# Start of a SwiGLU kernel: the four x chunks in three loads instead of four, used in another order

## The chip, the cores and the metric

The kernel runs on one core of a Trainium2 chip. The metric is the device time of one execution in microseconds, and the kernel is given the median over several runs. Besides the runs, one execution was recorded by the hardware profiler, and its views are what this document reads.

## The reference

The reference is a feed-forward layer with a gate. The inputs are bf16, and the sizes are 2048 rows of 640 values and a hidden width of 1536.

```python
B, S, D, F = 1, 2048, 640, 1536
g = silu(x @ w_gate)          # (S, F)
u = x @ w_up                  # (S, F)
return (g * u) @ w_down       # (S, D)
```

## The kernel before

All weights and the transposed x stay in the on-chip memory SBUF. The 2048 rows are worked on in four blocks (`sb`) of 512 rows, the hidden width in twelve columns of 128 (`fc`), and the contraction over 640 in five steps of 128 (`kd`). For each block and each `fc`, `proj` does five matmuls of 512 columns into the PSUM tile `pg` (gate) and five into `pu` (up), both on line 134. ScalarE computes `sg = silu(pg)` (line 180), and VectorE multiplies it by `pu` into `aT` (line 181). When a block's twelve columns are done, the down projection follows: the last 128 output columns first, transposed (`po_t`, line 189), and then 512 columns for each of four groups of rows (`po_a`, line 213). Then the next block begins.

The change lies in the first five microseconds, before that regular stream. The matmuls need x with the contraction dimension on the partitions. The blocks 1 to 3 get that by transposing loads (line 97). Block 0 would come too late that way, so its 512 rows are loaded plainly as four chunks of 128 rows (`load_x`, line 74, into `x_sb`). TensorE transposes each chunk in five 128x128 pieces (`transpose_chunk`, line 125) into a PSUM tile `pt`, and VectorE or ScalarE copies `pt` to `xT` (line 130). `pt` takes its space from the tags `po_a` and `po_b`, which have two buffers each. So the third tile of a tag waits until the copy of its first has freed the buffer.

Loads go out on two queues, SyncE's (`nc.sync`) and ScalarE's (`nc.scalar`). SyncE loads the chunks 0 and 1, and ScalarE the chunks 2 and 3. Behind them come the first 128 columns of `w_gate` and of `w_up`, each in two halves over the two queues (line 87). Then SyncE alone loads the further slices named by `W_CHUNKS` (line 71), gate and up by turns: columns 1 to 2 of `fc` (the second gate slice and the second up slice), then 3 to 5, 6 to 8 and 9 to 11. `w_down` and the transposed blocks of x follow. ScalarE also runs one small `Silu` (line 89), which makes it load its activation table early.

TensorE fills its waits with matmuls of ones into an unused tile (`warm`, line 103): `N_WARM` of them while x is on its way, `N_GAP` after the first two chunks, and two ahead of the first projection. The first gate projection goes over 256 columns at a time (`proj_pair`, line 149). Its first half takes the chunks 0 and 2 and its second half the chunks 1 and 3, since chunks 0 and 2 are the first loads of the two queues. `keep_order` holds TensorE's and ScalarE's instructions up to this point to the order in which they are written.

Of the kernel before, what the change touches and what calls it, by code (L numbers as in the profile page):

```python
# [10 lines left out]
def _body(  # L11
# [8 lines left out]
    nc = tc.nc  # L20
    P = nc.NUM_PARTITIONS
# [11 lines left out]
    KD = D // P  # L33
    KF = F // P
    S_BLK = 512
    NSB = S // S_BLK
    SUB = S_BLK // P
    DA = 512
    Q = 32
    N_WARM, N_GAP = 18, 4  # L40
    W_CHUNKS = [(0, 1), (1, 3), (3, 6), (6, 9), (9, 12)]
    assert D % P == 0 and F % P == 0 and S % S_BLK == 0 and D > DA and SUB == 4

# [9 lines left out]
    xT = consts.tile([P, KD, S], bf16)  # L53
    wg_sb = consts.tile([P, KD, F], bf16)
# [18 lines left out]
    def load_x(eng, c0, c1):  # L73
        eng.dma_start(out=x_sb[:, c0:c1, :], in_=x_v[:, c0:c1, :])
# [4 lines left out]

    queues = (nc.sync, nc.scalar)  # L80
    halves = ((0, KD // 2 + 1), (KD // 2 + 1, KD))
    for c in (0, 1):
        for i, eng in enumerate(queues):
            load_x(eng, c + 2 * i, c + 2 * i + 1)
    for dst, src in ((wg_sb, wg_v), (wu_sb, wu_v)):
        for eng, (k0, k1) in zip(queues, halves):
            eng.dma_start(out=dst[:, k0:k1, wslice(0, 1)], in_=src[:, k0:k1, wslice(0, 1)])
# [13 lines left out]
    def warm(n):  # L101
        for _ in range(n):
            nc.tensor.matmul(  # L103
                pw[:, 0:P], lhsT=ones[:], rhs=ones[:], start=True, stop=True
            )

    def keep_order(engine):

        traced = [i for i in nc.cur_bb.bb.instructions if i.engine == engine]
        for a, b in zip(traced, traced[1:]):  # L110
            tc.add_manual_dep(
                b,
                a.name,
                mybir.DependencyInfo(
                    mybir.DependencyClass.NoSync, mybir.DependencyReason.DATA
                ),
                reason="keep_order",
            )

    def transpose_chunk(c, parts):  # L120
        c_sl = slice(c * P, (c + 1) * P)
        for copy, tag, k0, k1 in parts:
            pt = psum.tile([P, k1 - k0, P], bf16, tag=tag, name="pt")
            for kd in range(k0, k1):
                nc.tensor.transpose(  # L125
                    out=pt[:, kd - k0, :],
                    in_=x_sb[:, c, kd * P : (kd + 1) * P],
                    identity=ident[:],
                )
            copy(out=xT[:, k0:k1, c_sl], in_=pt[:])  # L130

    def proj(ps, w_sb, fc, sb, c0, c1):
        for kd in range(KD):
            nc.tensor.matmul(  # L134
                ps[:, c0:c1],
                lhsT=w_sb[:, kd, fc * P : (fc + 1) * P],
                rhs=xT[:, kd, sb * S_BLK + c0 : sb * S_BLK + c1],
                start=(kd == 0),
                stop=(kd == KD - 1),
            )  # L140

    def proj_pair(ps, w_sb, fc, sb, b):


        def pair(ap):
            return ap.rearrange("p (a b c) -> p b a c", b=2, c=P)[:, b]

        for kd in range(KD):
            nc.tensor.matmul(  # L149
                pair(ps[:]),  # L150
                lhsT=w_sb[:, kd, fc * P : (fc + 1) * P],
                rhs=pair(xT[:, kd, sb * S_BLK : (sb + 1) * S_BLK]),
                start=(kd == 0),
                stop=(kd == KD - 1),
            )

    for sb in range(NSB):
        s_sl = slice(sb * S_BLK, (sb + 1) * S_BLK)
        for fc in range(KF):
            pg = psum.tile([P, S_BLK], f32, tag="gu", name="pg", bufs=4)  # L160
            pu = psum.tile([P, S_BLK], f32, tag="gu", name="pu", bufs=4)
            if sb == 0 and fc == 0:
                dve, act = nc.vector.tensor_copy, nc.scalar.copy
                warm(N_WARM)
                transpose_chunk(0, [(dve, "po_a", 0, KD)])
                transpose_chunk(2, [(dve, "po_b", 0, KD)])
                warm(N_GAP)
                for c in (1, 3):
                    transpose_chunk(c, [(act, "po_a", 0, 2), (dve, "po_b", 2, KD)])
                warm(2)  # L170
                proj_pair(pg, wg_sb, fc, sb, 0)
                proj_pair(pg, wg_sb, fc, sb, 1)
                proj(pu, wu_sb, fc, sb, 0, S_BLK)
                keep_order(mybir.EngineType.PE)
                keep_order(mybir.EngineType.Activation)
            else:
                proj(pg, wg_sb, fc, sb, 0, S_BLK)
                proj(pu, wu_sb, fc, sb, 0, S_BLK)
            sg = work.tile([P, S_BLK], f32)
            nc.scalar.activation(sg[:], pg[:], ACT.Silu)  # L180
            nc.vector.tensor_tensor(  # L181
                out=aT[:, fc, s_sl], in0=sg[:], in1=pu[:], op=ALU.mult
            )


        n_t = (SUB if sb < NSB - 1 else SUB - 1) * P
        po_t = psum.tile([P, n_t], f32, tag="po_b", name="po_t")
        for kf in range(KF):
            nc.tensor.matmul(  # L189
                po_t[:],  # L190
                lhsT=wd_sb[:, kf, DA:D],
                rhs=aT[:, kf, sb * S_BLK : sb * S_BLK + n_t],
                start=(kf == 0),
                stop=(kf == KF - 1),
            )
        ot_t = outp.tile([P, n_t], bf16, name="ot_t")
        ot_q = outp.tile([P, n_t], bf16, name="ot_q")
        nc.scalar.copy(ot_t[:], po_t[:])  # L198
        nc.vector.transpose(out=ot_q[:], in_=ot_t[:])  # L199
        for q in range(P // Q):  # L200
            nc.scalar.dma_start(
                out=out2[
                    sb * S_BLK : sb * S_BLK + n_t, DA + q * Q : DA + (q + 1) * Q
                ].rearrange("(i r) c -> r i c", r=Q),
                in_=ot_q[q * Q : (q + 1) * Q, :].rearrange("r (i c) -> r i c", c=Q),
            )

        for j in range(SUB):
            s0 = sb * S_BLK + j * P
            last = sb == NSB - 1 and j == SUB - 1  # L210
            po_a = psum.tile([P, DA], f32, tag="po_a", name="po_a")
            for kf in range(KF):
                nc.tensor.matmul(  # L213
                    po_a[:],
                    lhsT=aT[:, kf, s0 : s0 + P],
                    rhs=wd_sb[:, kf, 0:DA],
                    start=(kf == 0),
                    stop=(kf == KF - 1),
                )
            ot = outp.tile([P, DA], bf16, name="ot")  # L220
            nc.scalar.copy(ot[:], po_a[:])  # L221
            nc.sync.dma_start(out=out2[s0 : s0 + P, 0:DA], in_=ot[:])
            if last:
                po_b = psum.tile([P, D - DA], f32, tag="po_b", name="po_b")
                for kf in range(KF):
                    nc.tensor.matmul(  # L226
                        po_b[:],
                        lhsT=aT[:, kf, s0 : s0 + P],
                        rhs=wd_sb[:, kf, DA:D],
                        start=(kf == 0),  # L230
                        stop=(kf == KF - 1),
                    )
                ot_b = outp.tile([P, D - DA], bf16, name="ot_b")
                nc.vector.tensor_copy(out=ot_b[:], in_=po_b[:])  # L234
                nc.scalar.dma_start(out=out2[s0 : s0 + P, DA:D], in_=ot_b[:])
# [76 lines left out]
def kernel(tc, *args):  # L312
    _body(tc, *args)
    tc.close()
    tc.compile()
    _trim(tc.nc)
# [30 lines left out]
```

## Time and profile before

| what | value |
|---|---|
| median of 7 runs | 164.7 us |
| lowest and highest run | 163.99 and 164.94 us |
| the profiled execution: own time | 164.14 us |
| the profiled execution: span from first to last instruction | 162.8 us |
| TensorE matmul busy | 159.4 us, 98% of the span |
| ScalarE busy, VectorE busy | 42.4 us, 37.9 us |
| x loads of 160 KB: issue to landing, least, median, most | 2.5, 2.8, 3.3 us |
| second gate slice, 320 KB: issue to landing | 4.3 us |
| second up slice, 320 KB: issue to landing | 4.9 us |
| one 512-column matmul, one 256-column matmul | 379 ns, 274 ns |

Times in the views of the trace count from the start of the span. A duration of a matmul contains the time in the pipeline, and the next matmul starts before it ends. So the distance of two starts (the pitch) is what a matmul costs in a stream. In the views "PE" is the matmul side of TensorE and "PEld" its weight loads, which run ahead of the matmuls. "SPq" and "ACTq" are the DMA issues on SyncE's and ScalarE's queues; the length of such a row is the time of issuing, not of the transfer. "DVE" is VectorE and "ACT" ScalarE. An idle time in brackets is that of the row's engine just ahead of the row, with what ended it.

### The profile page before, as it was taken

What the parts mean: (1) busy time and instruction counts of PE and PEld (TensorE: products, weight loads), DVE (VectorE), ACT (ScalarE), POOL (GpSimd) and SP (SyncE); (2) the same over time, 40 slices, a digit from 0 to 9 for tenths busy, and PEclk for the clock granted to TensorE, in tenths of its full rate; (3) what the DMA queues carried; (4) which work ended last, traced back from release to release, by engine and by line L of the source; (5) the groups of instructions that cost most, each with busy time, mean ns of one, the idle gap of its engine ahead of it and who ended that gap; (6) DMA issues with size and microseconds to landing.
All of it is one profiled execution on the core that took longest, in us unless ns stands there. A gap on an engine that the chain in (4) does not pass through costs nothing.

```text
span 162.8 us, 1869 instructions
## 1 busy us (share of the span) xinstructions
PE 159.4 (98%) x766; PEld 75.3 (46%) x781; DVE 37.9 (23%) x58; ACT 42.4 (26%) x72; POOL 0.6 (0%) x6
## 2 busy tenths in 40 slices
PE   8999999999999999999999999999999999999994
PEld 8544444444444444444444444444444444445442
DVE  2322333310022333311002333331001333332000
ACT  3322222112222222221222222221213222222121
POOL 1000000000000000000000000000000000000000
PEclk9999999999999999999999999999999999999999
DMA  7999999804100000003110000000320000000302
GB/s 221 281 330 330 362 181 231 162 9 81 44 32 0 0 0 0 4 0 34 64 64 0 2 4 0 0 0 5 60 68 32 0 0 0 0 0 4 55 33 73
DMA packets 26888, 11.26 MB, mean 69 GB/s; under 512 B 17664, under 2 KB 26880, under 8 KB 26880
## 3 DMA queue, kind: packets, MB, share of 16 engines
q1 hardware_dynamic: 17968, 10.16, 23.5%
q10 hardware_dynamic: 8912, 0.98, 3.9%
q8 instruction: 6, 0.10, 0.3%
q14 instruction: 2, 0.02, 0.0%
HBM read 6.55 MB, written 2.62 MB: 56 GB/s over the span
## 4 chain that ended last, share of the span: by engine, by line
PE 94%; DMA 4%; issue 1%; DVE 0%
PE pg L134 31%; PE pu L134 31%; PE po_a L213 25%; PE po_t L189 6%; DMA wg_sb<-in_w_gate_dram 3%; DMA x_sb<-in_x_dram 2%; PE po_b L226 0%; DVE ot_b L234 0%
## 5 line engine op out<-in xcount | busy, mean ns | idle before, releaser
L134 PE MATMUL pu<-xT,wu_sb 128*128 128x512 bf16 x230 | 58.9, 379 | 0.5
L134 PE MATMUL pg<-xT,wg_sb 128*128 128x512 bf16 x235 | 58.4, 379 | 0.1
L181 DVE TENSOR_TENSOR aT<-sg,pu 128x512 bf16<-128x512 f32 x48 | 33.1, 689 | 100.9 <-PE pu L134 100.9
L180 ACT ACTIVATE sg<-pg 128x512 f32<-128x512 f32 x48 | 28.7, 597 | 71.6 <-PE pg L134 70.3
L213 PE MATMUL po_a<-wd_sb,aT 128*128 128x512 bf16 x188 | 41.9, 379 | 0.2
L134 PEld LDWEIGHTS <-wu_sb 128*128 128x128 bf16 x240 | 23.4, 98 | 28.2 <-DMA wu_sb<-in_w_up_dram 0.3
L134 PEld LDWEIGHTS <-wg_sb 128*128 128x128 bf16 x235 | 22.9, 98 | 28.1 <-DMA wg_sb<-in_w_gate_dram 0.6
L213 PEld LDWEIGHTS <-aT 128*128 128x128 bf16 x192 | 18.8, 98 | 22.6
L221 ACT CAST ot<-po_a 128x512 bf16<-128x512 f32 x16 | 9.4, 586 | 32.3 <-PE po_a L213 19.3
L189 PE MATMUL po_t<-aT,wd_sb 128*128 128x512 bf16 (+1 forms) x47 | 10.3, 365 | 0.1
L189 PEld LDWEIGHTS <-wd_sb 128*128 128x128 bf16 x48 | 4.7, 98 | 5.1
L198 ACT CAST ot_t<-po_t 128x512 bf16<-128x512 f32 (+1 forms) x4 | 2.2, 560 | 11.6 <-PE po_t L189 11.6
L199 DVE STREAM_TRANSPOSE ot_q<-ot_t 128x512 bf16<-128x512 bf16 (+1 forms) x4 | 2.7, 678 | 9.1 <-ACT ot_t L198 9.1
L103 PE MATMUL pw<-ones 128*128 128x128 bf16 x24 | 2.8, 290 | 0.4 <-DVE ones L78 0.4
L234 DVE CAST ot_b<-po_b 128x128 bf16<-128x128 f32 x1 | 0.3, 292 | 9.9 <-PE po_b L226 9.9
L103 PEld LDWEIGHTS <-ones 128*128 128x128 bf16 x24 | 2.3, 137 | 0.4 <-DVE ones L78 0.4
L130 DVE COPY xT<-pt 128x640 bf16<-128x640 bf16 (+1 forms) x4 | 1.7, 424 | 3.0 <-PE pt L125 3.0
L125 PE MATMUL pt<-ident,x_sb 128*128 128x128 bf16 x20 | 2.1, 263 | 0.0
L89 ACT ACT_TABLE_LOAD x1 | 1.3, 1283 | 2.0 <-issue 2.0
L125 PEld LDWEIGHTS <-x_sb 128*128 128x128 bf16 x20 | 1.6, 119 | 0.4 <-DMA x_sb<-in_x_dram 0.3
L149 PE MATMUL pg<-xT,wg_sb 128*128 128x256 bf16 x10 | 1.3, 274 | 0.0
L149 PEld LDWEIGHTS <-wg_sb 128*128 128x128 bf16 x10 | 0.9, 97 | 0.3 <-DMA wg_sb<-in_w_gate_dram 0.2
(11 smaller groups left out, 3.5 us busy)
## 6 DMA issues: line engine op xcount, KB each, us to landing
out_dram<-ot SPq DMA_DIRECT2D x16, 128.0 KB, 1.7
wd_sb<-in_w_down_dram SPq DMA_DIRECT2D x1, 1920.0 KB, 12.8
wg_sb<-in_w_gate_dram SPq DMA_DIRECT2D x3, 480.0 KB, 7.5
wu_sb<-in_w_up_dram SPq DMA_DIRECT2D x3, 480.0 KB, 7.4
out_dram<-ot_q ACTq DMA_DIRECT2D x12, 32.0 KB, 1.9
x_sb<-in_x_dram SPq DMA_DIRECT2D x2, 160.0 KB, 2.7
x_sb<-in_x_dram ACTq DMA_DIRECT2D x2, 160.0 KB, 3.0
wg_sb<-in_w_gate_dram SPq DMA_DIRECT2D x1, 320.0 KB, 4.3
```

The costliest lines, as they stand in the source:

```text
L103: nc.tensor.matmul(pw[:, 0:P], lhsT=ones[:], rhs=ones[:], start=True, stop=True)
L125: nc.tensor.transpose(out=pt[:, kd - k0, :], in_=x_sb[:, c, kd * P : (kd + 1) * P], identity=ident[:],)
L130: copy(out=xT[:, k0:k1, c_sl], in_=pt[:])
L134: nc.tensor.matmul(ps[:, c0:c1], lhsT=w_sb[:, kd, fc * P : (fc + 1) * P], rhs=xT[:, kd, sb * S_BLK + c0 : sb * S_BLK + c1], start=(kd == 0 ...
L149: nc.tensor.matmul(pair(ps[:]), lhsT=w_sb[:, kd, fc * P : (fc + 1) * P], rhs=pair(xT[:, kd, sb * S_BLK : (sb + 1) * S_BLK]), start=(kd == ...
L180: nc.scalar.activation(sg[:], pg[:], ACT.Silu)
L181: nc.vector.tensor_tensor(out=aT[:, fc, s_sl], in0=sg[:], in1=pu[:], op=ALU.mult)
L189: nc.tensor.matmul(po_t[:], lhsT=wd_sb[:, kf, DA:D], rhs=aT[:, kf, sb * S_BLK : sb * S_BLK + n_t], start=(kf == 0), stop=(kf == KF - 1),)
L198: nc.scalar.copy(ot_t[:], po_t[:])
L199: nc.vector.transpose(out=ot_q[:], in_=ot_t[:])
L213: nc.tensor.matmul(po_a[:], lhsT=aT[:, kf, s0 : s0 + P], rhs=wd_sb[:, kf, 0:DA], start=(kf == 0), stop=(kf == KF - 1),)
L221: nc.scalar.copy(ot[:], po_a[:])
```

## The change

SyncE loads chunk 0 and chunk 1 singly as before, and ScalarE loads the chunks 2 and 3 in one load of 320 KB. TensorE transposes the chunks in the order 0, 1, 2, 3 instead of 0, 2, 1, 3. The warm matmuls after the first chunks become three between chunk 0 and chunk 1 and two between chunk 1 and chunk 2, instead of four after the second chunk. Chunk 1 instead of chunk 2 is copied whole by VectorE, and chunk 2 instead of chunk 1 is copied in two parts, by ScalarE and VectorE. The first gate projection is done by `proj` on columns 0 to 255 and then 256 to 511, and `proj_pair` is gone. The loads of the weights, their order and everything after the first projection stay.

```diff
-    N_WARM, N_GAP = 18, 4
+    N_WARM, N_GAP = 18, 3
...
-    for c in (0, 1):
-        for i, eng in enumerate(queues):
-            load_x(eng, c + 2 * i, c + 2 * i + 1)
+    load_x(nc.sync, 0, 1)
+    load_x(nc.scalar, 2, SUB)
+    load_x(nc.sync, 1, 2)
...
-    def proj_pair(ps, w_sb, fc, sb, b):
...
                 transpose_chunk(0, [(dve, "po_a", 0, KD)])
-                transpose_chunk(2, [(dve, "po_b", 0, KD)])
                 warm(N_GAP)
-                for c in (1, 3):
+                transpose_chunk(1, [(dve, "po_b", 0, KD)])
+                warm(2)
+                for c in (2, 3):
                     transpose_chunk(c, [(act, "po_a", 0, 2), (dve, "po_b", 2, KD)])
                 warm(2)
-                proj_pair(pg, wg_sb, fc, sb, 0)
-                proj_pair(pg, wg_sb, fc, sb, 1)
+                proj(pg, wg_sb, fc, sb, 0, 2 * P)
+                proj(pg, wg_sb, fc, sb, 2 * P, S_BLK)
                 proj(pu, wu_sb, fc, sb, 0, S_BLK)
```

More of the change, by code (lines that the diff above doesn't have):

```diff
@@ L140, in proj @@
             )
-    def proj_pair(ps, w_sb, fc, sb, b):
[L145 to L155, printed above, removed]
     for sb in range(NSB):
```

## The prediction

> **What bounds the kernel now.** I read the shares of busy time first, then the weight-load waits of TensorE, then the start of the timeline queue by queue. The page gives the bound:
>
> ```profile
> PE 159.4 (98%) x766; PEld 75.3 (46%) x781; DVE 37.9 (23%) x58; ACT 42.4 (26%) x72; POOL 0.6 (0%) x6
> ```
>
> TensorE is occupied for nearly the whole span, and in the table of windows the stretch 7.24 to 26.00 shows 18.71 us of it busy out of 18.76. So whatever the change is worth lies before the first 512-column matmul that is followed by an unbroken stream, and the end moves by as much as that matmul moves. The timeline of weight loads from 3.4 to 8.4 us shows where TensorE still waits:
>
> ```profile
> 4.79 0.99 PEld L149 LDWEIGHTS <-wg_sb 128*128 128x128 bf16 x10 [0.17 <-DMA wg_sb<-in_w_gate_dram]
> 5.79 0.85 PEld L134 LDWEIGHTS <-wu_sb 128*128 128x128 bf16 x5
> 7.24 0.76 PEld L134 LDWEIGHTS <-wg_sb 128*128 128x128 bf16 x5 [0.59 <-DMA wg_sb<-in_w_gate_dram]
> ```
>
> Columns are start, length, what it is, and in brackets the idle time before it with its releaser. Weight loads run ahead of matmuls, so 0.59 us of idle weight loading is not 0.59 us of lost TensorE. The lost part comes from the matmuls of the same stretch:
>
> ```profile
> 4.79 1.26 PE L149 MATMUL pg<-xT,wg_sb 128*128 128x256 bf16 x10
> 6.11 1.03 PE L134 MATMUL pu<-xT,wu_sb 128*128 128x512 bf16 x4
> 7.24 1.25 PE L134 MATMUL pg<-xT,wg_sb 128*128 128x512 bf16 x5
> 8.33 1.24 PE L134 MATMUL pu<-xT,wu_sb 128*128 128x512 bf16 x5
> ```
>
> Four of the five first pu matmuls are recorded (the first is missing). The last begins at 6.11 + 1.03 - 0.38 (one takes 379 ns) = 6.76. The pitch is (1.25 - 0.38)/4 = 0.216, so the next could begin at 6.98 and begins at 7.24: **0.26 us lost** to the second gate slice. The second up slice costs 8.33 - (7.24 + 5 x 0.216) = 0.01. Ahead of the first projection 0.17 is lost to the first gate slice. All data waits between 4.6 and 8.4 are thus 0.44 us, 0.27% of the time. Why the second gate slice is late stands in SyncE's queue and its waits:
>
> ```profile
> 0.00 0.86 SPq L74 DMA_DIRECT2D x_sb<-in_x_dram  x2
> 0.91 0.43 SPq L87 DMA_DIRECT2D wg_sb<-in_w_gate_dram  x1
> 1.39 0.49 SPq L87 DMA_DIRECT2D wu_sb<-in_w_up_dram  x1
> 2.90 0.37 SPq L71 DMA_DIRECT2D wg_sb<-in_w_gate_dram  x1
> ```
>
> ```profile
> SPq L71 <- DMA x_sb<-in_x_dram: 1.0, 1, 1.0
> ```
>
> The queue is free at 1.88 and stands until 2.90, when an x load lands (the second fence: total, times and longest wait). Eight loads stand ahead of it over both queues (four of x, four weight halves), and the ninth is held by an early one[...]. The chain of waits runs through the same point:
>
> ```profile
> 0.12 2.77 DMA x_sb<-in_x_dram
> 2.88 0.02 issue
> 2.90 4.29 DMA wg_sb<-in_w_gate_dram
> 7.20 0.04 issue
> 7.24 1.25 PE pg L134 x5
> ```
>
> So the holder is the ScalarE load of chunk 2, issued at 0.12 and landed at 2.88. The late issue leaves a hole in the transfers; the table of windows (length, busy engines, TensorE clock, DMA share, GB/s) shows it between two full stretches:
>
> ```profile
> 4.00:4.50 0.50, 0.50 (x10) 0.41 (x8) 0.49 (x2) 0.36 (x2) 0.00 (x0) 1.00 1.17 248
> 4.50:5.00 0.50, 0.50 (x7) 0.32 (x6) 0.45 (x2) 0.29 (x2) 0.00 (x0) 1.00 0.72 118
> 5.00:5.50 0.50, 0.50 (x7) 0.44 (x6) 0.07 (x1) 0.00 (x0) 0.00 (x0) 1.00 1.06 254
> ```
>
> 118 GB/s against some 250 on either side: about half of 0.5 us, 0.27 us of transfer time, is lost.
>
> [...]with start plus time to landing, the x chunks land at 2.5 (0, SyncE), 2.9 (2, ScalarE), 3.3 (1, SyncE) and 3.85 (3, ScalarE), in turns, a whole load each, although chunk 1 was issued at 0.45. [...]18 warm matmuls from 0.40 take 2.10 us, a pitch of (2.10 - 0.31)/17 = 0.105, and from about 3.6 the same shape goes at 0.056 (four transposes from 3.83 in 0.39 us).[...]
>
> **The change part by part.**
> *Second gate slice eighth.* One load fewer stands ahead, so it is issued at about 1.9 instead of 2.90. Its data then queue directly behind the first up slice. The hole of 0.27 us closes, so it lands at 6.93 at the latest, and up to 1.0 earlier (6.2) if the issue time passes through whole. Either is under the 6.98 at which TensorE could use it: **-0.26 us**, and -0.01 for the up slice, which moves with it. That is worth nothing more, because TensorE is next limited by its own pitch.
> *The ninth load* is now the second up slice, and it inherits the wait, probably on the ScalarE load, which now carries chunks 2 and 3 (landing 3.3 to 3.85). It is issued between 3.35 and 3.9, before 3.31. Behind it on SyncE stand only the later slices, of which the next lands at 3.88 + 5.8 = 9.7 and is used after 11.5. I take its cost as zero: the gate slice's 320 KB occupy the transfers until about 5.5, and with the hole closed it lands at 8.26 - 0.27 = 7.99, before 8.06. If the delay passes whole, it lands at 8.85.
> *One x load fewer on ScalarE.* An issue takes 0.41 to 0.45 us; the two weight halves and the activation-table load (2.05 to 3.33) move up by that. ScalarE's next need is its copy at 4.14, so 0. Bytes ahead of the first gate slice stay the same, so I leave its landing at 4.75; bounds -0.1 to +0.1.
> *One warm matmul more* (3 + 2 against 4): 0.06 to 0.105 us, inside waits on loads, 0.
> *Halves instead of pairs.* Both are ten 256-column matmuls at a 0.109 pitch; their first half now needs chunks 0 and 1. 0.
> *The order of x.* Now chunk 1 is needed second, and in turns of whole loads it comes third.[...] Taken whole, chunks 2 and 3 land at about 3.3 and chunk 1 at 3.85. Cut in two turns, chunk 1 keeps 3.3. This isn't shown before; the bounds are these two landings. I take 3.85, since the trace shows whole loads alternating. Then: chunk 0 and three warm matmuls end at 2.54 + 8 x 0.105 = 3.37; TensorE stands until 3.89; the last of five transposes begins at 4.11; VectorE's copy follows 0.26 later (as 4.46 to 4.72 before) and takes 0.49, to 4.86. Meanwhile TensorE runs two warm matmuls, chunk 2 and two of chunk 3, to 4.67. The other three need the po_b buffer that this copy frees: 4.90. Three transposes and two warm ones later, at 5.18, the first projection starts, against 4.79: **+0.39 us**. VectorE's last copy ends at 5.63, before the second half needs it at 5.73.
> *Sum:* +0.39 - 0.27 = **+0.12 us** on the profiled execution (164.14 us; span 162.8 and 1.3 around it). That execution is the second fastest of seven; the median is 164.7, so the forecast is 164.8.
>
> **The rivals.**
> *Forecast, 0.45:* the sum above; no change, 164.8, own range 164.3 to 165.2. A measurement here tells about 0.3% (0.5 us) from no change.
> *Chunk 1 lands at 3.3, 0.30:* then its transposes start at 3.37, chunk 2's at 3.9, the last copy is where it was, the first projection starts at 4.79 and the whole 0.27 is gained: 164.4. For it: chunk 1 is issued at 0.45. With the 0.17 wait gone as well the gain is 0.44: 164.25.
> *The clock steps up late, 0.15, slower:* with chunk 1 at 3.85 TensorE idles for 0.5 us at 3.37 to 3.89[...]. Transposes at 0.105 bring the first projection to 5.89; five of its matmuls go at 0.213, the rest at 0.109, to 7.54; pu takes 1.08; the second gate projection starts at 8.62 instead of 7.24: +1.4 us, 166.1.[...] It decides once the step comes later than about 5.2.
> *A wait takes the other's place, 0.10, slower:* the count is not what holds the slice, and it waits for the double load (3.85 instead of 2.88): +1.0, 165.7. Or the up slice lands at 8.85: +0.56, 165.3.
>
> **How the numbers follow.** The range 164.1 to 165.9 holds the first two cases with the bounds of their landings and most of the last; beyond it lies a late clock. The medians of runs from 163.99 to 164.94 wander by some 0.2 us. Faster by over 0.3%: half of the second case and a little of the first, 0.2. Slower: most of the last two, and a seventh of the first, 0.26. Same: 0.54.
>
> **What would show it.** SyncE's second gate slice issued near 1.9; no wait on wg_sb at the second gate projection; a wait of about 0.5 us on x_sb ahead of chunk 1's transposes; the first projection at 5.2; two pitches, changing near 3.6. It is wrong if chunk 1 lands before the double load, if the pitch stays at 0.105 past 4.5, or if a wait on wu_sb appears near 8.

## The result, and the profile after

The changed kernel is **slower**: median of 15 runs 166.37 us (164.39 to 166.99) against 164.48 us for the kernel before (38 runs, 163.88 to 164.94), measured beside it. The ratio is 1.0092, with a 95% interval of 1.0070 to 1.0114. Here and below a run more than 1.5% above the fastest of its kernel counts in the median but not in the ratio. The forecast was 164.8 with a range to 165.9, so the result lies outside it. It is the third case of the prediction, the late clock step, which had 166.1 and a chance of 0.15. The profiled execution took 166.49 us (span 165.2), 2.35 us over the one of before. That is more than the 1.9 us between the medians, because the profile of before caught one of its faster executions.

The page's first line of busy time looks almost as before, and hides the loss:

```profile
PE 161.0 (97%) x767; PEld 76.8 (47%) x782; DVE 37.9 (23%) x58; ACT 42.5 (26%) x72; POOL 0.6 (0%) x6
```

SyncE's queue, from the timeline of its issues, shows that the change does what it says. The second gate slice goes out at 1.91 instead of 2.90, and the second up slice has taken its wait:

```profile
0.00 0.86 SPq L74 DMA_DIRECT2D x_sb<-in_x_dram  x2
...
1.91 0.49 SPq L71 DMA_DIRECT2D wg_sb<-in_w_gate_dram  x1
3.48 0.37 SPq L71 DMA_DIRECT2D wu_sb<-in_w_up_dram  x1
```

The gate slice lands at 1.91 + 4.7 = 6.6 instead of 7.20. The up slice lands at 3.48 + 4.4 = 7.9. The hole in the transfers is gone too. This is the row of the table of windows that had 118 GB/s before:

```profile
4.50:5.00 0.50, 0.50 (x8) 0.50 (x6) 0.20 (x1) 0.00 (x0) 0.00 (x0) 1.00 1.20 240
```

So the transfers behaved as planned, and the loss is on TensorE. Its timeline:

```profile
2.83 0.53 PE L103 MATMUL pw<-ones 128*128 128x128 bf16 x3
4.05 0.71 PE L125 MATMUL pt<-ident,x_sb 128*128 128x128 bf16 x5 [0.69 <-DMA x_sb<-in_x_dram]
4.56 0.42 PE L103 MATMUL pw<-ones 128*128 128x128 bf16 x2
4.77 1.27 PE L125 MATMUL pt<-ident,x_sb 128*128 128x128 bf16 x10
5.84 0.42 PE L103 MATMUL pw<-ones 128*128 128x128 bf16 x2
6.05 2.34 PE L134 MATMUL pg<-xT,wg_sb 128*128 128x256 bf16 x10
8.61 1.18 PE L134 MATMUL pu<-xT,wu_sb 128*128 128x512 bf16 x4 [0.22 <-issue]
9.63 1.24 PE L134 MATMUL pg<-xT,wg_sb 128*128 128x512 bf16 x5
```

Two things stand here. TensorE idles for 0.69 us before chunk 1's transposes. Then everything runs at half speed for a long time: the ten 256-column matmuls take 2.34 us where they took 1.26, a pitch of (2.34 - 0.42)/9 = 0.213 instead of 0.109. Only within the first up projection does the pitch change: four recorded matmuls fit into 1.18 us, and from 9.63 the pitch is 0.216 again. The last of the four begins at 8.61 + 1.18 - 0.38 = 9.41, so two of the three distances are at full speed (0.216) and the first, 0.37, is between: the pitch halved near 8.9 instead of 3.6. This is the prediction's late clock step. The views show it in the pitch alone; that a clock stands behind it is the author's reading. The "0.22 <-issue" ahead of pu is no wait; the first pu matmul is missing from the records, as it was before.

The table of windows gives no hint of this. Its clock column says 1.00 for the same stretch (length, busy and count of PE, PEld, DVE, ACT and POOL, clock, DMA share, GB/s):

```profile
3.36:4.05 0.69, 0.00 (x1) 0.00 (x1) 0.21 (x1) 0.00 (x0) 0.00 (x0) 1.00 1.27 284
6.05:8.20 2.15, 2.15 (x12) 1.53 (x12) 0.36 (x1) 0.09 (x1) 0.00 (x0) 1.00 1.12 304
```

The step has to be read from the distance of equal matmuls; the column and the busy share both look full.

The chain of waits has changed its carrier. Before it ran through chunk 2's load and the second gate slice; now it runs through chunk 1's load and on through TensorE's own work:

```profile
0.45 3.55 DMA x_sb<-in_x_dram
4.01 0.05 issue
4.05 0.71 PE pt L125 x5
```

The 2.39 us between the starts of the second gate projection (9.63 against 7.24) divide as follows. The first projection starts at 6.05 instead of 4.79: +1.26. Its ten matmuls take ten pitches, 2.13 instead of 1.09: +1.04. From there to the second gate projection it is 1.45 instead of 1.36: +0.09, in which the lost wait of 0.26 is hidden by the half-speed matmuls. From there on the two executions stay the same distance apart (spans 165.2 and 162.8).

### The profile page after: what moved, and what is told of

It reads as the page before. It is cut to its first block, busy times and chain, and to the rows that moved or that the text cites. A ratio compares the mean times of both kernels' runs of the same rounds, so it can differ in the third digit from the quotient of the medians.

```text
span 165.2 us, 1870 instructions
## 1 busy us (share of the span) xinstructions
PE 161.0 (97%) x767; PEld 76.8 (47%) x782; DVE 37.9 (23%) x58; ACT 42.5 (26%) x72; POOL 0.6 (0%) x6
## 4 chain that ended last, share of the span: by engine, by line
PE 96%; DMA 2%; issue 1%; SPq 0%; DVE 0%
PE pg L134 32%; PE pu L134 31%; PE po_a L199 25%; PE po_t L175 6%; DMA x_sb<-in_x_dram 2%; PE pt L125 1%; PE po_b L212 0%; PE pw L103 0%; SPq L74 0%; DVE ot_b L220 0%
## 5 line engine op out<-in xcount | busy, mean ns | idle before, releaser
L134 PE MATMUL pg<-xT,wg_sb 128*128 128x512 bf16 (+1 forms) x245 | 60.7, 381 | 0.0
L134 PEld LDWEIGHTS <-wg_sb 128*128 128x128 bf16 x245 | 24.5, 100 | 28.2
L199 PEld LDWEIGHTS <-aT 128*128 128x128 bf16 x192 | 18.8, 98 | 22.5
L103 PE MATMUL pw<-ones 128*128 128x128 bf16 x25 | 3.5, 313 | 0.4 <-DVE ones L78 0.4
L125 PE MATMUL pt<-ident,x_sb 128*128 128x128 bf16 x20 | 2.7, 311 | 0.7 <-DMA x_sb<-in_x_dram 0.7
L130 ACT COPY xT<-pt 128x256 bf16<-128x256 bf16 x2 | 0.7, 372 | 2.3 <-PE pt L125 2.3
L212 PEld LDWEIGHTS <-aT 128*128 128x128 bf16 x12 | 0.8, 98 | 0.2
```

The costliest lines, as they stand in the source:

```text
L103: nc.tensor.matmul(pw[:, 0:P], lhsT=ones[:], rhs=ones[:], start=True, stop=True)
L125: nc.tensor.transpose(out=pt[:, kd - k0, :], in_=x_sb[:, c, kd * P : (kd + 1) * P], identity=ident[:],)
L134: nc.tensor.matmul(ps[:, c0:c1], lhsT=w_sb[:, kd, fc * P : (fc + 1) * P], rhs=xT[:, kd, sb * S_BLK + c0 : sb * S_BLK + c1], start=(kd == 0 ...
L199: nc.tensor.matmul(po_a[:], lhsT=aT[:, kf, s0 : s0 + P], rhs=wd_sb[:, kf, 0:DA], start=(kf == 0), stop=(kf == KF - 1),)
```

## The experiments

Each kernel was timed beside the kernel before, so the ratios are to be compared, not the medians of different experiments. The theory: the 0.69 us in which the change lets TensorE idle make the clock step come late. The rivals: the late landing and the new order alone cost the time, or the loads do.

**The hole filled.** The changed kernel with more warm matmuls where it waits.

```diff
-    N_WARM, N_GAP = 18, 3
+    N_WARM, N_GAP = 18, 11
```

> The changed kernel with eleven instead of three warm matmuls between chunk 0 and chunk 1, so that TensorE has work until chunk 1 lands near 4.0 us. Loads and all else as in the change. Theory[...]: no hole over 0.2 us[...], median 164.4 to 165.0, that is 1.5 us below the change's 166.4. Rival (the time goes with the late landing of chunk 1 and the order of the work alone, not with idleness): the first projection starts where it did and the median stays at 166 to 166.7. Rival (the early gate slice or the longer ScalarE load slows something later): stays at 166 to 166.7 too, with the clock stepping up early.

Median 164.69 us, all 22 runs between 164.41 and 165.25; ratio 1.0022 (1.0010 to 1.0033). With the loads and the order of the change untouched, eight matmuls that compute nothing take away most of the loss: 0.70 of 0.92% by the ratios, 1.5 of 1.9 us by the medians. The timeline of TensorE:

```profile
2.82 1.38 PE L103 MATMUL pw<-ones 128*128 128x128 bf16 x11
4.19 0.71 PE L125 MATMUL pt<-ident,x_sb 128*128 128x128 bf16 x5
...
5.76 1.25 PE L134 MATMUL pg<-xT,wg_sb 128*128 128x256 bf16 x10
```

Chunk 1 is as late as in the change (4.19), yet the first projection runs at full speed, a pitch of (1.25 - 0.27)/9 = 0.109. What remains, 0.22% or some 0.4 us, is the net of everything else in the change. Two delays show in this execution. Chunk 1 comes late, and the second up slice, which took over the wait for its issue, isn't free here: the second up projection begins at 9.21, when it could have begun at 7.93 + 1.08 = 9.01. The weight loads show that wait:

```profile
9.21 0.76 PEld L134 LDWEIGHTS <-wu_sb 128*128 128x128 bf16 x5 [0.53 <-DMA wu_sb<-in_w_up_dram]
```

**An early hole in the kernel before.** Nothing is changed but the number of warm matmuls.

```diff
-    N_WARM, N_GAP = 18, 4
+    N_WARM, N_GAP = 10, 4
```

> The kernel before with 10 instead of 18 warm matmuls at the start: nothing changes in loads or order, only TensorE idles for some 0.8 us before chunk 0 lands. Theory:[...] median 165.5 to 166.5, spread up to 167, and a step near 5.5 to 9 us in the profile. Rival (order and landings are the cause): 164.5, as before, since those warm matmuls compute nothing.

Median 165.00 us (164.29 to 165.82), ratio 1.0038 (1.0023 to 1.0053): slower, as the theory has it and the rival not, but by less than the 165.5 to 166.5 expected. Its timeline:

```profile
2.61 1.25 PE L125 MATMUL pt<-ident,x_sb 128*128 128x128 bf16 x10 [0.96 <-DMA x_sb<-in_x_dram]
...
5.36 2.34 PE L149 MATMUL pg<-xT,wg_sb 128*128 128x256 bf16 x10
7.49 1.46 PE L134 MATMUL pu<-xT,wu_sb 128*128 128x512 bf16 x5
```

The hole of 0.96 us is longer than the change's, and the half-speed pitch (0.213) again covers the first projection, but the hole ends at 2.6 instead of 4.05, and the step comes sooner too. From 7.49 to the second gate projection at 8.79 it is 1.30 instead of five full-speed pitches, 1.08, so by estimate one pitch more went at half speed and the step came near 7.9 instead of 8.9. Whether the place of the hole makes that difference, this run alone does not show. A hole in a later place is tested next.

**A late hole in the kernel before, and the same filled.** The four single loads stay. TensorE takes the chunks in the order 0, 3, 1, 2, so that it waits for the last one; the pair differs only in nine warm matmuls.

```diff
                 transpose_chunk(0, [(dve, "po_a", 0, KD)])
-                transpose_chunk(2, [(dve, "po_b", 0, KD)])
                 warm(N_GAP)                 # N_GAP: 0, and 9 in the filled one
-                for c in (1, 3):
+                transpose_chunk(3, [(dve, "po_b", 0, KD)])
+                for c in (1, 2):
...
-                proj_pair(pg, wg_sb, fc, sb, 0)
-                proj_pair(pg, wg_sb, fc, sb, 1)
+                proj(pg, wg_sb, fc, sb, 0, S_BLK)
```

> The loads of the kernel before, all x chunks landing by 3.85 us, but TensorE takes them in the order 0, 3, 1, 2 with no warm matmul after chunk 0, so it idles from about 3.0 until chunk 3 lands near 3.85 to 4.0; the first gate projection is one of 512 columns. Theory[...]: median 165.8 to 166.6, some runs near 164.5. Rival (a hole costs 0.6 us, as the early one did, and the rest of the change's loss is the late chunk 1): 164.9 to 165.2.

> The same as e5_late_hole with nine warm matmuls after chunk 0, which fill the hole and compute nothing. Theory: median 164.4 to 164.9. Rival (the order 0, 3, 1, 2 costs the time): as e5_late_hole.

With the hole: median 166.29 us (166.00 to 167.13, six runs), ratio 1.0118 (1.0092 to 1.0145). Filled: 164.79 us (164.23 to 165.50), ratio 1.0020 (1.0008 to 1.0031). So a loss of the change's size appears with the loads of the kernel before: 1.0% between the two, where filling the hole of the change gained 0.7%. Some runs with the hole were expected near 164.5; of the six, none was. From the timeline of the kernel with the hole:

```profile
4.08 1.78 PE L125 MATMUL pt<-ident,x_sb 128*128 128x128 bf16 x15 [0.70 <-DMA x_sb<-in_x_dram]
...
6.00 2.29 PE L134 MATMUL pg<-xT,wg_sb 128*128 128x512 bf16 x5
```

and of the filled one:

```profile
4.23 1.81 PE L125 MATMUL pt<-ident,x_sb 128*128 128x128 bf16 x15
...
6.17 1.24 PE L134 MATMUL pg<-xT,wg_sb 128*128 128x512 bf16 x5
```

The filled kernel starts its first projection 0.17 us later and runs it in little more than half the time.

**How long a hole may be.** The changed kernel with five and seven warm matmuls instead of three.

```diff
-    N_WARM, N_GAP = 18, 3
+    N_WARM, N_GAP = 18, 7    # and 18, 5
```

> The changed kernel with seven instead of three warm matmuls between chunk 0 and chunk 1, so that the hole is about half as long (0.5 us from start to start instead of 1.0).[...] If only the larger hole is too much: as e1_fill, 164.7. In between, with runs of both kinds, if the tolerance lies near 0.3 us of idleness.

> The changed kernel with five instead of three warm matmuls between chunk 0 and chunk 1: two fewer than seven, at which all runs stayed under 165.5, two more than three, at which most are over 165.8. The idle time is near 0.5 to 0.6 us. Theory[...]: runs of two kinds, near 164.8 and near 166.5, and few between; the median at one of the two. Rival (lost time grows with the hole): runs of one kind near 165.5.

With seven: 164.82 us, no run over 165.49; ratio 1.0022 (1.0011 to 1.0034). With five: 164.67 us, 21 runs from 164.43 to 165.32 and one at 166.67, none between; ratio 1.0026 (1.0009 to 1.0043). The idle times, from the timeline of the one with seven and then of the one with five:

```profile
4.31 0.46 PE L125 MATMUL pt<-ident,x_sb 128*128 128x128 bf16 x5 [0.45 <-DMA x_sb<-in_x_dram]
```

```profile
4.20 0.72 PE L125 MATMUL pt<-ident,x_sb 128*128 128x128 bf16 x5 [0.56 <-DMA x_sb<-in_x_dram]
```

Taken with the change (0.69 us idle; 11 of 15 runs over 165.5) this looks like a step and not a slope. With 0.45 us no run is long, with 0.56 one of 22, and with 0.69 most. A loss that grows with the hole would have put the kernel with five near 165.5, and its median is 164.67. So runs of two kinds, as the theory expected, fit. The idle times come from one profile each, though. They vary with the landing of chunk 1, whose transposes begin at 4.05 in the change, at 4.20 with five and at 4.31 with seven, and how long the hole was in the one long run isn't known.

**The order alone.** Four single loads as before, the change's order on TensorE and its halves; then the same with seven warm matmuls after chunk 0.

```diff
-    load_x(nc.sync, 0, 1)
-    load_x(nc.scalar, 2, SUB)
-    load_x(nc.sync, 1, 2)
+    for c in (0, 1):
+        for i, eng in enumerate(queues):
+            load_x(eng, c + 2 * i, c + 2 * i + 1)
```

> The four single x loads of the kernel before, with the change's order on TensorE (0, three warm, 1, two warm, 2, 3, contiguous halves). Chunk 1 then lands near 3.3 as before. Theory: no hole, median within 0.3 us of 164.5. Rival (the order of the compute part or the halves cost the time, whatever the loads): near 166.

> e4_compute_only (four single x loads, the change's order on TensorE) with seven instead of three warm matmuls after chunk 0. In e4_compute_only four of 22 runs lay at 166.2 to 166.8 and the rest under 165.0. Theory (those four had a hole before chunk 1[...], because chunk 1 came late in them): no run over 165.5. Rival (they come from something else in the order or the halves): some runs over 166 again.

The first: 164.58 us, ratio 1.0014 (0.9998 to 1.0030), but four of 22 runs lie at 166.2 to 166.8 and the others under 165.0. The filled one: 164.41 us, ratio 1.0009 (0.9994 to 1.0024), all 14 runs under 164.9. The ratio of the first leaves three of these four out; by the means of all runs it is 1.0030. Where nothing idles, the order and the halves cost nothing that can be measured. That the four runs had a longer hole is only suggested: 14 runs without one could be chance, and no profile caught such a run.

**The loads of the change, taken as they land.** TensorE transposes 0, 2, 3, 1, and the first gate projection begins with the second half of the columns.

```diff
-    N_WARM, N_GAP = 18, 3
+    N_WARM, N_GAP = 18, 6
...
-                transpose_chunk(1, [(dve, "po_b", 0, KD)])
-                warm(2)
-                for c in (2, 3):
+                transpose_chunk(2, [(dve, "po_b", 0, KD)])
+                for c in (3, 1):
...
-                proj(pg, wg_sb, fc, sb, 0, 2 * P)
                 proj(pg, wg_sb, fc, sb, 2 * P, S_BLK)
+                proj(pg, wg_sb, fc, sb, 0, 2 * P)
```

> The loads of the change, but TensorE takes the chunks as they land: 0, six warm matmuls, 2, 3, 1, and the first gate projection does columns 256 to 511 first. Theory: TensorE has no hole over 0.2 us, the clock steps as in the kernel before, and the early second gate slice gives up to 0.27 us, of which a later landing of the first gate slice (5.0 instead of 4.75) may take back all: median 164.1 to 164.7. Rival (the loads themselves cost the time): 166 or more.

Median 164.35 us, ratio 1.0006 (0.9993 to 1.0020): no loss from the loads, and no gain from the early gate slice. The timeline shows where the gain went:

```profile
3.60 0.84 PE L125 MATMUL pt<-ident,x_sb 128*128 128x128 bf16 x12
4.63 0.33 PE L125 MATMUL pt<-ident,x_sb 128*128 128x128 bf16 x3 [0.19 <-DVE xT L130]
...
4.91 1.26 PE L134 MATMUL pg<-xT,wg_sb 128*128 128x256 bf16 x10
...
7.08 1.24 PE L134 MATMUL pg<-xT,wg_sb 128*128 128x512 bf16 x5
```

From the first to the second gate projection it is 2.17 instead of 2.45 us, so the wait is gone; but the first starts at 4.91 instead of 4.79. Its weights aren't what holds it: they landed at 0.91 + 3.9 = 4.8, and TensorE comes to it without a pause. The last three transposes waited 0.19 us for a copy of VectorE to free their PSUM buffer. What is left of the gain, 0.16 us, is under what the runs can tell.

**Two other ways to make the gate slice the eighth load.** In one, x stays and the first up slice is a single load on SyncE; in the other, the merged x load stands second on SyncE and chunk 1 goes first on ScalarE, so that the chunks land in the order of use.

```diff
-    for dst, src in ((wg_sb, wg_v), (wu_sb, wu_v)):
-        for eng, (k0, k1) in zip(queues, halves):
-            eng.dma_start(out=dst[:, k0:k1, wslice(0, 1)], in_=src[:, k0:k1, wslice(0, 1)])
+    for eng, (k0, k1) in zip(queues, halves):
+        eng.dma_start(out=wg_sb[:, k0:k1, wslice(0, 1)], in_=wg_v[:, k0:k1, wslice(0, 1)])
+    load_w(nc.sync, wu_sb, wu_v, *W_CHUNKS[0])
```

> The kernel before with the first up slice as one load on SyncE instead of two halves, so that the second gate slice is the eighth load without touching x or TensorE's order. Theory (the wait of 0.26 us for that slice is real and the early issue removes it): issued near 1.9, landed by 6.9, up to 0.27 us faster in runs with an early clock step and less in the others, median 0.1 to 0.27 under the kernel before. Rival (in the middling run TensorE comes later than the slice anyway): no difference.

```diff
-    N_WARM, N_GAP = 18, 3
+    N_WARM, N_GAP = 18, 5
...
-    load_x(nc.scalar, 2, SUB)
-    load_x(nc.sync, 1, 2)
+    load_x(nc.scalar, 1, 2)
+    load_x(nc.sync, 2, SUB)
...
-                warm(N_GAP)
                 transpose_chunk(1, [(dve, "po_b", 0, KD)])
-                warm(2)
+                warm(N_GAP)
```

> Three x loads as in the change, but chunk 1 goes alone on ScalarE as its first load and the merged load of chunks 2 and 3 goes second on SyncE, so that the chunks land in the order in which TensorE takes them (0, 1, five warm matmuls, 2, 3). Theory: chunk 1 lands near 2.9, 2 and 3 near 3.9 to 4.1, no hole over 0.3 us, the second gate slice is issued near 1.9 and lands by 6.9. The clock steps as in the kernel before; of the 0.26 us wait the runs with an early step gain up to all, the others less: median 0 to 0.25 under the kernel before. Rival (three x loads as such cost something, wherever they stand): 0.3 us or more over it.

The first: 164.48 us, ratio 0.9997 (0.9983 to 1.0012). The second: 164.53 us, ratio 1.0011 (0.9994 to 1.0028). Neither can be told from the kernel before, so the gain that was expected of both doesn't show. For the second the interval also leaves room for up to 0.28% of loss. In the first, the wait has moved to the first up slice, which now lands at 1.39 + 5.0 = 6.4 instead of 1.39 + 4.0 = 5.4:

```profile
6.44 1.25 PE L134 MATMUL pu<-xT,wu_sb 128*128 128x512 bf16 x5 [0.49 <-DMA wu_sb<-in_w_up_dram]
```

In the second, the merged load lands at 0.45 + 3.9 = 4.35, after TensorE has done all else:

```profile
4.41 0.90 PE L125 MATMUL pt<-ident,x_sb 128*128 128x128 bf16 x10 [0.31 <-DMA x_sb<-in_x_dram]
```

No version beats both kernels.

## Why the prediction was wrong

**The transfers: right, but for one term put at nothing.** The issue at 1.9, the vanished wait on the second gate slice, the closed hole of 118 GB/s and the wait inherited by the second up slice all came as worked out. That the inherited wait costs nothing holds in the change's profile, where TensorE is late anyway. In the profile with the hole filled it cost 0.2 us.

**The order of x: right, undersized.** In the change the merged load lands whole before chunk 1: near 3.47 (SyncE's up slice is released by it at 3.48) and at 4.01 (in the chain), against 3.3 and 3.85 in the sum. So chunk 1 came behind both chunks of the double load, as the sum had it. With seven warm matmuls chunk 1 came later still, its transposes beginning at 4.31 where the sum had 3.89. With the hole filled the whole change measured +0.22%, some 0.4 us, against the forecast sum of +0.12.

**The step that failed** is the price of the 0.5 us wait at chunk 1. The sum put it down as a delay of 0.39 us and left the step near 3.6. But 3.6 belongs to that one execution, and the place of the step in another can't be taken from it. Two kernels without a long hole, with the same 18 warm matmuls from 0.4 on, differ: in the one with the loads taken as they land, the twelve transposes from 3.60 on go at a pitch of 0.056, while in the filled version of the order alone the pitch is still 0.107 at 4.33 to 5.39:

```profile
4.33 1.27 PE L125 MATMUL pt<-ident,x_sb 128*128 128x128 bf16 x10
```

What sets the place of the step is not shown. Nor was the step late in every run of the change, as far as the times tell: 4 of its 15 stayed at 165.3 or below. What the runs show in place of the 0.39 us is the late step: filling the wait takes back 1.5 of the 1.9 us. With 11 of 15 runs over 165.5, the third case should have had the largest chance and not 0.15.

**The third case: right in kind, undersized.** It had the second gate projection at 8.62 (its own terms add up to 8.58) and the step after five matmuls of the first projection, at 5.89 + 5 x 0.213 = 6.96; the profile has 9.63 and about 8.9. How long the half speed would last after the idle time was shown by no view of before. In the change it lasted from 4.05 to about 8.9, 4.9 us, and in the kernel with the early hole from 2.61 to about 7.9, 5.3 us. On the median the case had +1.4, and +1.9 was measured (+1.5 by the ratio).

**The gain of 0.27 us: not seen even without the hole.** Five kernels issue the second gate slice early and have, in all their runs, none of the long times (the filled hole, the one with seven warm matmuls, the loads taken as they land, and the two other ways), and none is faster than the kernel before. In the last three the profile names what is late next: a copy of VectorE that holds the last transposes until 4.63, the first up slice at 6.4, the merged load at 4.35. There is also a doubt about the gain itself. The 0.26 us were read from a fast execution of before. In the kernel with the early hole, where the step comes late, near 7.9, the second gate projection starts 1.30 us after the first up projection (7.49 and 8.79) and shows no idle time ahead of it, with the loads of before, whose slice goes out at 2.90 and had cost 0.26 us. So a middling execution of before may have had less to gain; no profile of one was taken. In the change the merged load let the second gate slice go out at 1.91 instead of 2.90, and in return chunk 2 landed only with chunk 3, near 3.47 instead of 2.88.

## What to carry to other kernels

Ahead of a long run of matmuls, ask of each wait on TensorE not only how long it is but whether it comes before the pitch has halved (here from 0.213 to 0.109): 0.7 us of idleness in that time cost 1.5 us (166.29 against 164.79 for the same kernel with the hole filled), and nine matmuls of ones took that away. Warm matmuls belong behind the last work before each load, in the number that lasts until it lands, and a merge or a change of order among the first loads means counting them anew. Look at several runs too: two groups of times some 2 us apart, as in the order alone, say what one profile can't.

## What the runs showed of the hardware that was not expected

Little idleness is enough, and the bound is narrow: with 0.45 us in the profile no run of 22 was long, with 0.56 one of 22, with 0.69 (the change) 11 of 15, with 0.70 all six, where another 0.16 us of idleness stood ahead of chunk 0. The place seems to count as well: 0.96 us idle up to 2.6 cost 0.38%, 0.70 us up to 4.1 cost 1.0% (1.0118 against 1.0020 when filled). What decides which of the two kinds a run is stays open; only these points are measured. And a half-speed stretch shows neither in the busy share nor in the clock column of these views, but in the pitch (0.213 instead of 0.109) and so in the length of a group of matmuls.
